# Linear attention into a gated unit: sixteen small gate tiles, and q maxima subtracted without a mask

## The chip, the cores and the metric

The kernel runs on one core of a Trainium2 chip. The core has a matrix engine (TensorE, PE in the profile; its weight loads are shown apart as PEld), VectorE (DVE), ScalarE (ACT), GpSimd (POOL) and SyncE (SP), which here only issues transfers. The metric is the device time of one execution in microseconds (us), the median of several runs.

## The reference

The inputs are q, k and v of 8 batches, 8 heads, 576 positions and 64 channels, and a projection `w_phi` to 128 features. The first half is attention without a softmax over positions; the second half is a gated unit with a causal convolution of five taps over positions, whose 512 channels are the heads side by side.

```python
def phi(x):
    proj = np.einsum('bhsd,df->bhsf', x, w_phi)
    proj = proj - np.max(np.abs(proj), axis=-1, keepdims=True)
    return np.concatenate([np.exp(proj), np.exp(-proj)], axis=-1)
q_p, k_p = (phi(q), phi(k))
kv = np.einsum('bhsf,bhsd->bhfd', k_p, v)
z = np.sum(k_p, axis=2)
num = np.einsum('bhsf,bhfd->bhsd', q_p, kv)
den = np.einsum('bhsf,bhf->bhs', q_p, z)[..., None] + 1e-06
...
for k in range(K):
    gate_pre += conv_w[k][None, None, :] * xp[:, k:k + S, :]
gate = 1.0 / (1.0 + np.exp(-gate_pre))
val = x @ w_val
return (gate * val @ w_out).astype(np.float32)
```

## The kernel before

The batches run one after another through a chain of steps, and the steps of neighbouring batches overlap. Two positions (an even and an odd one) stand on the two halves of the 128 partitions, so most matmuls use 64 rows, in pairs on the two row halves. The 18 blocks of 128 positions and heads of a batch are taken in five units, four of four blocks and one of two (`UNITS`).

The steps of a batch, with the tiles they write:

- Loads: k and q go through `KQN` and a transposing transfer into `kT` and `qT` (batches 0 and 1: through TensorE, lines 537 and 556, with casts at 543, 545 and 561). v goes to `VN`. A one-element copy on GpSimd (`hold`, line 510) waits for the last q block of batch 0, and the loads behind it on GpSimd's queue wait with it.
- k: `kp` projects a unit (line 578), VectorE takes the maxima of the magnitudes (586, into `MK`), ScalarE the two exponentials (596, into `KTIL`). `ek` (605) makes the factors exp of plus and minus the maximum, and `vs` (611 and 612, GpSimd) multiplies v by them, into `VT`, with a column of factors for the denominator: four instructions of 18 x 64 elements a batch, one for each group of heads and sign. `st` (621) sums key features times scaled v into a state, `kv` evicts it (629 or 633, into `KV`).
- q: `qm` projects (578), VectorE takes maxima into `MQP` (586). `mqt` transposes them (663), `mqr` copies them negated into `MQR` (671). `rx` (683, GpSimd) spreads them over a mask of the identity, into `RX`. `qp` projects again (694) and adds, as a second matmul with weights of ones, `RX` (699), so that the maxima are subtracted in PSUM. ScalarE then takes the exponentials (707 and 710, into `QTIL` and `QTT`).
- `num` multiplies q features with the state (720, 727), `nrm` divides (738, 741, into `XN`), and x is transposed into `XT` (749, 753; in the last two batches by a transfer).
- The gated unit works on blocks j of 128 channels. `gate` (782) makes the convolution as matmuls with small diagonal matrices of taps, `GW`: for each tap four matmuls of 64 x 64 tiles, on two row halves and two column halves, for even and odd positions (`par`) in two PSUM banks. ScalarE takes a tanh (786, into `TH`). `val` (792) is the value matmul, `gv` (798) joins the two, and `out` (814, 818) multiplies with `WOUT`; the results are evicted by ScalarE (635) or VectorE (631) and written by SyncE.

Order is written out by hand in tables: `ORDER` lists the steps of all engines in the order in which they are issued, `FLEX` says for each step that can run on two engines which it takes, `BANKS` gives PSUM banks to groups. `WARM` and `ZERO` put extra matmuls into TensorE's stream: full-width ones on ones, and ones with weights of zero that add nothing to a unit's PSUM (line 505). The durations in `build` were for making these tables; they do not act on the chip.

Of the kernel before, what the change touches and what calls it, by code (L numbers as in the profile page):

```python
# [10 lines left out]
ALU = mybir.AluOpType  # L11
# [6 lines left out]
F = 128  # L18
# [6 lines left out]
NU = len(UNITS)  # L25
PEB = 1
QPART = ((0, 1), (2, 3, 4))
# [83 lines left out]
def dve(n, ov=0.075):  # L111
    return n / 960.0 + ov


def act(n):
    return n * 0.000833 + 0.067


class Plan:
    def __init__(self):  # L120
        self.tasks, self.groups = [], []

    def group(self, kind, nb):
# [35 lines left out]
def parts(b):  # L159
    return QPART if b == 0 else (tuple(range(NU)),)  # L160


def build(plan, em=None):
# [11 lines left out]
    def G(*k):  # L175
        return h.get(k)
# [725 lines left out]
```

## Time and profile before

| what | us |
|---|---|
| runs | 216.41, 217.7, 218.19 |
| median | 217.7 |
| span of the profiled execution | 216.2 |
| busy PE, ACT, DVE, POOL | 194.8, 180.8, 170.1, 133.1 |

The profiled execution has no time of its own beside its span; the lowest run is 0.2 us above that span, and the median 1.5 us. Busy time is the union of the instructions' times: matmuls overlap, and each counts with its whole latency, so that PE's busy share says more than its work. A row of the costliest groups gives line, engine, operation, output and inputs with their shape and the number of instructions, then busy time, mean duration in ns, and the idle time just before them with what ended it. A row of the timeline gives start, length and what ran, with like neighbours merged into one piece.

### The profile page before, as it was taken

Reading aid. Unit: us, or ns where it says so; the run is one execution under the profiler, and the core shown is the slowest. Engines: PE = TensorE matmul, PEld = TensorE weight load, DVE = VectorE, ACT = ScalarE, POOL = GpSimd, SP = SyncE. Lnnn points to the kernel's source line nnn. Section 1 sums busy time; section 2 is a strip of 40 time slices with the busy share of each in tenths; the row PEclk is TensorE's granted clock in tenths of the full one; section 3 lists DMA queues with packets and bytes.
Section 4 is the critical chain, followed back from the end, with each engine's and each line's share of the span. In section 5 each row is a group of like instructions: output and inputs, shape, how many; then the busy total and the mean of one; then the engine's idle time right before and its main releaser. Section 6 shows DMA issues by size and latency. Waiting matters only on the chain.

```text
span 216.2 us, 9004 instructions
## 1 busy us (share of the span) xinstructions
PE 194.8 (90%) x3924; PEld 139.5 (65%) x3944; DVE 170.1 (79%) x257; ACT 180.8 (84%) x267; POOL 133.1 (62%) x173
## 2 busy tenths in 40 slices
PE   2987978778999999998999999999999999899990
PEld 2665566566666776676857777568757766687740
DVE  2289999999599988997899978998699897654510
ACT  3689999999999899998999997999988988634251
POOL 3045999997894749961998099902993779210010
PEclk9999999999999999999999999999999999999998
DMA  6999999899599699979998968969953264774166
GB/s 180 380 242 208 306 169 238 154 195 196 111 167 299 115 137 235 300 138 184 220 311 150 137 137 233 199 141 178 296 190 89 62 163 129 85 169 94 49 193 198
DMA packets 49106, 39.86 MB, mean 184 GB/s; under 512 B 33637, under 2 KB 38565, under 8 KB 49066
## 3 DMA queue, kind: packets, MB, share of 16 engines
q1 hardware_dynamic: 42768, 28.58, 57.0%
q0 software_dynamic: 6032, 10.49, 26.1%
q8 instruction: 31, 0.51, 0.9%
q10 hardware_dynamic: 266, 0.21, 0.3%
q14 instruction: 9, 0.07, 0.1%
HBM read 30.48 MB, written 9.44 MB: 185 GB/s over the span
## 4 chain that ended last, share of the span: by engine, by line
PE 55%; ACT 22%; DVE 14%; issue 4%; DMA 2%; SPq 0%; DVEq 0%; ACTq 0%
PE PS L792 11%; PE PS L814 9%; ACT QTIL L707 9%; PE PS L782 9%; ACT KTIL L596 8%; DVE MQP L586 6%; PE PS L720 5%; PE PS L578 5%; PE PS L621 4%; DVE MK L586 3%; DMA KTIL<-in_k_dram 2%; PE PS L694 2%; PE PS L537 2%; PE PS L818 2%; PE PS L699 2%
## 5 line engine op out<-in xcount | busy, mean ns | idle before, releaser
L596 ACT ACTIVATE KTIL<-PS 128x1024 bf16<-128x1024 f32 (+1 forms) x80 | 71.8, 966 | 3.9 <-PE PS L578 1.7
L611 POOL TENSOR_TENSOR VT<-VN,EK 128x1152 bf16<-128x1152 f32 x32 | 67.9, 2121 | 3.3 <-ACT EK L605 3.2
L707 ACT ACTIVATE QTIL<-PS 128x1024 bf16<-128x1024 f32 x64 | 62.6, 1053 | 1.9 <-PE PS L699 1.5
L683 POOL TENSOR_TENSOR RX<-MQR,ident 128x512 bf16<-128x512 bf16 (+1 forms) x39 | 36.6, 961 | 36.7 <-DVE MQR L671 26.1
L586 DVE TENSOR_REDUCE MK<-PS 128x8 f32<-128x1024 f32 (+1 forms) x40 | 44.2, 1112 | 3.5 <-PE PS L578 1.7
L586 DVE TENSOR_REDUCE MQP<-PS 128x8 bf16<-128x1024 f32 (+1 forms) x40 | 43.7, 1112 | 2.7 <-PE PS L578 1.2
L792 PE MATMUL PS<-XT,WV 128*128 128x288 bf16 x256 | 34.8, 286 | 0.3 <-DVE GV L798 0.2
L798 DVE SCALAR_TENSOR_TENSOR GV<-TH,PS 128x576 bf16<-128x576 bf16 x32 | 23.8, 752 | 10.4 <-PE PS L792 4.7
L814 PE MATMUL PS<-WOUT,GV 128*128 128x512 bf16 x110 | 29.7, 380 | 1.1 <-issue 0.2
L792 PEld LDWEIGHTS <-WV 128*128 128x128 bf16 x256 | 23.8, 98 | 7.9 <-issue 1.4
L786 ACT ACTIVATE TH<-PS 128x576 bf16<-128x576 f32 x32 | 20.3, 664 | 8.9 <-PE PS L782 8.7
L621 PE MATMUL PS<-VT,KTIL 64*128 64x65 bf16 x1152 | 23.0, 191 | 0.8 <-issue 0.7
L782 PE MATMUL PS<-XT,GW 64*64 64x288 bf16 x640 | 23.0, 285 | 0.6 <-DVE RCP L738 0.5
L741 DVE TENSOR_TENSOR XN<-PS,RCP 128x512 bf16<-128x512 f32 x32 | 22.1, 691 | 1.2 <-DMA XT<-XN 0.2
L621 PEld LDWEIGHTS <-KTIL 64*128 64x128 bf16 x1152 | 20.7, 95 | 3.3 <-issue 2.3
L720 PEld LDWEIGHTS <-QTIL 128*128 128x128 bf16 x512 | 18.3, 97 | 6.4 <-issue 4.0
L720 PE MATMUL PS<-KV,QTIL 128*128 128x65 bf16 x512 | 20.3, 193 | 0.3 <-DVE MQP L586 0.2
L782 PEld LDWEIGHTS <-GW 64*64 64x64 bf16 x640 | 17.9, 106 | 3.0 <-issue 0.6
L635 ACT ACTIVATE OUTS<-PS 128x512 f32<-128x512 f32 x22 | 13.6, 621 | 7.3 <-PE PS L814 6.1
L814 PEld LDWEIGHTS <-GV 128*128 128x128 bf16 x128 | 11.2, 98 | 11.3 <-issue 0.6
L578 PE MATMUL PS<-W,qT 64*128 64x128 bf16 x288 | 15.4, 219 | 3.1 <-ACT QTIL L707 1.0
L578 PEld LDWEIGHTS <-qT 64*128 64x128 bf16 x288 | 10.8, 95 | 9.4 <-issue 4.6
(80 smaller groups left out, 236.0 us busy)
## 6 DMA issues: line engine op xcount, KB each, us to landing
out_dram<-OUTS SPq DMA_DIRECT2D x32, 256.0 KB, 3.3
VN<-in_v_dram SPq DMA_DIRECT2D x7, 1152.0 KB, 6.5
KQN<-in_q_dram POOLq DMA_DIRECT2D x6, 576.0 KB, 8.2
KQN<-in_k_dram POOLq DMA_DIRECT2D x6, 576.0 KB, 9.0
KTIL<-in_k_dram SPq DMA_DIRECT2D x4, 288.0 KB, 4.2
VN<-in_v_dram POOLq DMA_DIRECT2D x1, 1152.0 KB, 10.2
KTIL<-in_q_dram SPq DMA_DIRECT2D x4, 256.0 KB, 4.4
out_dram<-OUTS SPq DMA_DIRECT2D x14, 64.0 KB, 2.5
```

The lines of the kernel that those rows point to most:

```text
L578: nc.tensor.matmul(self.PS[:, t.grp.banks[par], i * P:(i + 1) * P], X[rows, (c0 + i) * P:(c0 + i + 1) * P], self.W2[rows, :], start=True, ...
L586: self.nc.vector.tensor_reduce(o, self.two(t.grp, n * P).rearrange("p a (c f) -> p a c f", f=F), AX.X, ALU.max, apply_absolute_value=True)
L596: self.nc.scalar.activation(self.KTIL[b % 2][:, s, c0:c0 + n, :, :].rearrange("p c a f -> p a c f"), self.two(t.grp, n * P).rearrange("p a ...
L611: nc.gpsimd.tensor_tensor(self.VT[g][:, s, :, 0:D], self.VN[b % 2][:, NC * g:NC * g + NC, :], e.to_broadcast([P, NC, D]), ALU.mult)
L621: nc.tensor.matmul(self.PS[:, t.grp.banks[ab], (s * 2 + x) * E1:(s * 2 + x + 1) * E1], self.KTIL[b % 2][rows, s, J // 2, J % 2, :], self.V ...
L683: self.nc.gpsimd.tensor_tensor(o, *wide(self.MQR[self.mq(b, u)][:, :], self.ident2), ALU.mult)
L707: self.nc.scalar.activation(o, i, AF.Exp, scale=1.0 - 2.0 * s)
L720: nc.tensor.matmul(self.PS[:, t.grp.banks[h // 4], (h % 4) * E1:(h % 4 + 1) * E1], Q[:, s, c % 2, h, (c // 2) * P:(c // 2 + 1) * P], self. ...
L782: self.nc.tensor.matmul(self.PS[o * D:(o + 1) * D, t.grp.banks[par], 0:R], self.GW[r, jj, 4 - m, :], X[r, 4 * a + jj, :, HALO - 8 * s:HALO ...
L792: self.nc.tensor.matmul(self.PS[:, t.grp.banks[par], 0:R], self.WV[:, i, (2 * j + par) * D:(2 * j + par + 2) * D], X[:, 4 * par + i, :, HA ...
L798: nc.vector.scalar_tensor_tensor(out=self.GV[b % 3][:, j, :, :], in0=self.TH[j][:, :, :], scalar=1.0, in1=self.two(t.grp, R), op0=ALU.add, ...
L814: nc.tensor.matmul(self.PS[:, t.grp.banks[0], :], GV[:, j, c % 2, (c // 2) * XH:(c // 2) * XH + P], self.WOUT[:, c % 2, j, :], start=(j == ...
```

## The change

Five parts, and new tables.

1. `gate` works on two channel blocks at once. Each tap is now sixteen matmuls of 32 x 32 tiles, on four row strips and four column strips, for two blocks (`z`) and even and odd positions (`par`); each (z, par) has its own PSUM bank, so a double gate holds four banks. The channels of a block come out rotated by 32 for odd blocks and by 64 for odd positions, and the value and output weights are rotated to match: `WVE` and `WVO` are rotated copies of the value weights, made by four GpSimd copies, and `WOUT` is loaded in three transfers instead of one, with two copies within the chip instead of three.
2. `rx` and its tile are gone. `qp` subtracts the maxima by four narrow matmuls (two in the last unit) on each row half: the moving operand is `MQR` itself, and the weights are one column of the identity read with a stride of zero, which picks one row of `MQR` for all 128 outputs.
3. `vs` is cut by key half x instead of by sign: one instruction scales 9 positions by both factors. `st` of a half waits for its own `vs` alone. It may run on VectorE; one of 32 does.
4. `mqr` may run on ScalarE; two of nine do.
5. `ZERO` is empty: the 150 matmuls with zero weights are gone. `WARM` now puts six full-width matmuls at the very start, and four later.

```diff
 WARM = (
-    "60:6:1 81:1:1 87:7:2 134:7:1 141:7:1 "
+    "2:6:6 103:0:2 161:3:1 185:3:1 "
 )
-ZERO = "35:76:7 61:80:5 75:34:1 101:105:1 126:215:8 144:223:1 155:192:4 158:200:1 175:315:6 189:346:1 195:241:2 197:241:2 211:327:1"
+ZERO = (
+    ""
+)
 ORDER = (
-    "1 2 9 3 4 11 5 6 10 21 22 19 20 13 12 46 25 26 7 8 23 24 14 27 28 42 29 32 30 33 44 49 76 31 15 43 45 47 16 158 159 48 "
+    "1 2 9 10 3 4 0 11 21 22 32 12 33 46 47 5 6 42 44 45 76 27 28 7 8 77 13 15 48 17 19 20 30 14 43 23 24 25 26 50 16 54 49 "
...
     def c_wv(self, t):
-        self.nc.gpsimd.dma_start(self.WV[:, :, 0:DM], self.wts[0].rearrange("(i p) o -> p i o", p=P))
-
-    def c_wvx(self, t):
-        self.nc.gpsimd.tensor_copy(self.WV[:, :, DM:DM + D], self.WV[:, :, 0:D])
+        self.nc.gpsimd.dma_start(self.WV[:, :, :], self.wts[0].rearrange("(i p) o -> p i o", p=P))
+
+    def c_wvx(self, t, odd):
+        cp = self.nc.gpsimd.tensor_copy
+        W = self.WV[:, :, :].rearrange("p i (w z c) -> p i w z c", w=2, z=2)[:, :, :, odd, :]
+        if odd:
+            cp(self.WVO[:, :, :, 0:96], W[:, :, :, 32:P])
+            cp(self.WVO[:, :, :, 96:192], W[:, :, :, 0:96])
+        else:
+            cp(self.WVE[:, :, :, 0:D], W[:, :, :, D:P])
+            cp(self.WVE[:, :, :, D:P], W[:, :, :, 0:D])
...
-    def vs(self, t, b, g, s):
-        nc = self.nc
-        e = self.EK[:, s, NC * g:NC * g + NC].unsqueeze(2)
+    def vs(self, t, b, g, x):
+        nc = self.nc
+        eng = nc.gpsimd if t.eng == "POOL" else nc.vector
+        r = slice(9 * x, 9 * x + 9)
+        e = self.EK[:, :, NC * g + 9 * x:NC * g + 9 * x + 9].unsqueeze(3)
+        v = self.VN[b % 2][:, NC * g + 9 * x:NC * g + 9 * x + 9, :].unsqueeze(1)
         with nc.allow_low_precision("bf16 scaled v"):
-            nc.gpsimd.tensor_tensor(self.VT[g][:, s, :, 0:D], self.VN[b % 2][:, NC * g:NC * g + NC, :], e.to_broadcast([P, NC, D]), ALU.mult)
-            nc.gpsimd.tensor_copy(self.VT[g][:, s, :, D:E1], e)
+            eng.tensor_tensor(self.VT[g][:, :, r, 0:D], v.to_broadcast([P, 2, 9, D]), e.to_broadcast([P, 2, 9, D]), ALU.mult)
+            eng.tensor_copy(self.VT[g][:, :, r, D:E1], e)
...
-        o = self.RX[u][:, :, 0:n, :]
-        if t.eng == "POOL":
-            self.nc.gpsimd.tensor_tensor(o, *wide(self.MQR[self.mq(b, u)][:, :], self.ident2), ALU.mult)
...
     def qp(self, t, b, u):
...
-        for par in range(2):
-            rows = slice(par * D, (par + 1) * D)
-            nc.tensor.matmul(self.PS[:, t.grp.banks[par], 0:n * P].rearrange("p (h y x) -> p h y x", h=2 * H, y=n),
-                             self.ONES[rows, 0:F], self.RX[u][rows, :, 0:n, :], start=False, stop=True, skip_group_check=True)
+        for y in range(n):
+            for par in range(2):
+                rows = slice(par * D, (par + 1) * D)
+                o = self.PS[:, t.grp.banks[par], 0:n * P].rearrange("p (h y x) -> p h y x", h=2 * H, y=n)
+                nc.tensor.matmul(o[:, :, y, :], self.ident2[rows, c0 + y:c0 + y + 1].to_broadcast([D, F]),
+                                 M[rows, :].rearrange("p (h x) -> p h x", h=2 * H), start=False, stop=True, skip_group_check=True)
...
-    def gate(self, t, b, j):
+    def gate(self, t, b, w):
         X = self.XT[b % 2]
         for m in range(5):
-            for h2 in range(2):
-                r = slice(h2 * D, (h2 + 1) * D)
-                for par in range(2):
-                    o = (h2 + par) % 2
-                    back = m - par
-                    s, a, jj = (back + 1) // 2, back % 2, (j + (par > h2)) % 4
-                    self.nc.tensor.matmul(self.PS[o * D:(o + 1) * D, t.grp.banks[par], 0:R], self.GW[r, jj, 4 - m, :],
-                                          X[r, 4 * a + jj, :, HALO - 8 * s:HALO - 8 * s + XH], start=(m == 0), stop=(m == 4))
+            for z, par in ((0, 0), (1, 0), (0, 1), (1, 1)):
+                j = 2 * w + z
+                bank = (t.grp, t.also)[z].banks[par]
+                back = m - par
+                s, a = (back + 1) // 2, back % 2
+                for i in range(4):
+                    o = (i - 2 * par - z) % 4
+                    r = slice(32 * i, 32 * i + 32)
+                    self.nc.tensor.matmul(self.PS[32 * o:32 * o + 32, bank, 0:R], self.GW[r, j, 4 - m, :],
+                                          X[r, 4 * a + j, :, HALO - 8 * s:HALO - 8 * s + XH], start=(m == 0), stop=(m == 4))
```

The tables move work in all engines. First place: the start of GpSimd's queue, from the `hold` copy (written to `HOLD`) on, before:

```order
L510 CAST HOLD_76<-KTIL1_73 128x1
L551 DMA QTIL1_75<-in_q_dram 128x2304
L551 DMA QTIL1_75<-in_k_dram 128x4x576
L551 DMA KQN1_65<-in_q_dram 128x2304
L551 DMA KQN0_64<-in_k_dram 128x4x576
L683 TENSOR_TENSOR RX1_135<-MQR0_90,ident2_130 128x512
L683 TENSOR_TENSOR RX0_134<-MQR0_90,ident2_130 128x512
L532 DMA VN1_67<-in_v_dram 128x4x576
L611 TENSOR_TENSOR VT0_82<-VN0_66,EK_86 128x18x64
L612 CAST VT0_82<-EK_86 128x18
```

The same place now:

```order
L544 DMA VN1_67<-in_v_dram 128x4x576
L522 CAST HOLD_76<-KTIL1_73 128x1
L563 DMA QTIL1_75<-in_q_dram 128x2304
L563 DMA QTIL1_75<-in_k_dram 128x4x576
L563 DMA KQN1_65<-in_q_dram 128x2304
L563 DMA KQN0_64<-in_k_dram 128x4x576
L626 TENSOR_TENSOR VT0_82<-VN0_66,EK_86 128x2x9x64
L627 CAST VT0_82<-EK_86 128x2x9
```

The load of batch 1's v went from behind two `rx` to ahead of the hold, with nothing but memsets before it; the `rx` are gone.

Second place: the start of ScalarE, casts of k and q of batch 0 (`kT0`, `qT0`) and the first exponentials (`KTIL0`), before:

```order
L456 DMA cw5_141<-in_moe_conv_w_dram 5x512
L545 ACT_TABLE_LOAD
L545 CAST kT0_68<-PS_63 128x512 x3
L596 ACTIVATE KTIL0_72<-PS_63 128x2x4x128 x2
L545 CAST qT0_70<-PS_63 128x512
```

And now:

```order
L454 DMA cw5_141<-in_moe_conv_w_dram 5x512
L557 ACT_TABLE_LOAD
L557 CAST kT0_68<-PS_63 128x512
L557 CAST qT0_70<-PS_63 128x512
L608 ACTIVATE KTIL0_72<-PS_63 128x2x4x128 x3
```

Two casts of k went to VectorE here, one cast of q came ahead of the exponentials; in all, ScalarE has five of these ten casts instead of nine.

Third place: ScalarE after the last q exponentials (`QTT`), with the tanh of the last two batches (`TH`), before:

```order
L710 ACTIVATE QTT_81<-PS_63 128x8x32 x4
L635 ACTIVATE OUTS7_118<-PS_63 128x512
L786 ACTIVATE TH3_105<-PS_63 128x576
L786 ACTIVATE TH2_104<-PS_63 128x576
L786 ACTIVATE TH0_102<-PS_63 128x576
L633 COPY XT1_101<-PS_63 128x16x16
L786 ACTIVATE TH1_103<-PS_63 128x576
```

And now:

```order
L714 ACTIVATE QTT_81<-PS_63 128x8x32 x4
L648 COPY XT0_103<-PS_63 128x16x16
L650 ACTIVATE OUTS7_121<-PS_63 128x512
L792 ACTIVATE TH3_108<-PS_63 128x576
L792 ACTIVATE TH2_107<-PS_63 128x576
L792 ACTIVATE TH1_106<-PS_63 128x576
L792 ACTIVATE TH0_105<-PS_63 128x576
```

The last transposed piece of batch 6's x is now copied here too, and the tanh come in pairs, as two are fed by one double gate. Behind the last q exponential TensorE had eight gates, eight value groups and nine output groups; now it has four double gates, eight value groups and eleven output groups.

More of the change, by code (lines that the diff above doesn't have):

```diff
@@ L116, in act, with parts @@
     return n * 0.000833 + 0.067
+def parts(b):
+    return QPART if b == 0 else (tuple(range(NU)),)
 class Plan:
@@ L224, in build @@
                 cx = A("lk", 0, 0, "DMA", 3.7, None, [cl], rank=-450)
-                cx = A("wvx", 0, 0, "POOL", 0.4, fn("c_wvx"), [cx], rank=-440)
-                cx = A("wvx", 0, 0, "DMA", 0.0, None, [cx], rank=-440)
+                cx = [A("wvx", 0, i, "POOL", 1.4, fn("c_wvx", i), [cx], rank=-440) for i in range(2)]
             last = [xf["q"], xf["k"]]
@@ L249, in build @@
             cc = A("mqt", 0, 0, "DVE", 0.2, fn("c_cw2"), [cc], g, rank=-500)
[L250 to L252 removed]
+            cg = A("mqt", 0, 0, "POOL", 1.3, fn("c_gt"), [cc], rank=-10)
             for j in range(4):
[L254 to L255 removed]
+                h["val", 0, j].deps.append(cx[j % 2])
+            for j in (0, 2):
+                h["gate", 0, j].deps.append(cg)
         ld = h["lv0",] = A("lv", b, 0, "POOL" if b == 1 else "SP", 0.65, fn("loadv", b),
@@ L276, in build @@
         for gi in range(2):
-            for s in range(2):
-                h["vs", b, gi, s] = A("vs", b, gi, "POOL", 2.22, fn("vs", b, gi, s),
-                                      [eks[gi % len(eks)], G("lv", b)] + [G("st", b - 1, gi, x) for x in range(2)])
+            for x in range(2):
+                h["vs", b, gi, x] = A("vs", b, gi, ("POOL", "DVE"), (2.22, 1.36), fn("vs", b, gi, x),
+                                      [eks[gi % len(eks)], G("lv", b), G("st", b - 1, gi, x)])
             g = plan.group("st", 2)
@@ L335, in build @@
         xall = [G("xtc", b, i) for i in range(3)] + [halo]
-        for j in range(4):
-            g = plan.group("gate", 2)
-            gt = h["gate", b, j] = A("gate", b, j, "PE", 0.62, fn("gate", b, j), xall, g, 3)
-            h["tanh", b, j] = A("tanh", b, j, "ACT", act(576), fn("tanh", b, j), [gt, G("gv", b - 1, j)], g)
+        for w in range(2):
+            gs = [plan.group("gate", 2) for _ in range(2)]
+            gt = A("gate", b, w, "PE", 0.66, fn("gate", b, w), xall, gs[0], 3, also=gs[1])
+            for i in range(2):
+                j = 2 * w + i
+                h["gate", b, j] = gt
+                h["tanh", b, j] = A("tanh", b, j, "ACT", act(576), fn("tanh", b, j), [gt, G("gv", b - 1, j)], gs[i])
         for j in range(4):
@@ L404, in __init__ @@
         self.MQR = TT("MQR", 3, [P, P])
+        for m in self.MQP:
+            nc.gpsimd.memset(m[:, :], 0.0)
         self.KV = TT("KV", 2, [P, 2, 2, 2, 2, E1])
```

89 lines of the change are left out of this document (39 added, 50 removed), and 67 rows, old and new, of the table ORDER.

## The prediction

> **What bounds the kernel now.** I read the page's totals first, then the chain of work that ended last, then busy time by stretch, then ScalarE's waits, and last the tail.
>
> ```profile
> span 216.2 us, 9004 instructions
> PE 194.8 (90%) x3924; PEld 139.5 (65%) x3944; DVE 170.1 (79%) x257; ACT 180.8 (84%) x267; POOL 133.1 (62%) x173
> PE 55%; ACT 22%; DVE 14%; issue 4%; DMA 2%; SPq 0%; DVEq 0%; ACTq 0%
> ```
>
> The chain is more than half TensorE (PE), and GpSimd (POOL) is not in it. Busy time by stretch (columns: length, then PE, weight loads, VectorE, ScalarE, GpSimd):
>
> ```profile
> 13.00:43.00 30.00, 24.12 (x543) 17.63 (x540) 28.30 (x37) 28.89 (x45) 24.27 (x26) 1.00 1.05 214
> 100.00:186.00 86.00, 84.99 (x1758) 59.65 (x1768) 75.50 (x116) 78.69 (x117) 60.95 (x74) 1.00 0.79 170
> 186.00:217.00 31.00, 24.44 (x349) 17.00 (x350) 11.57 (x21) 11.43 (x21) 2.18 (x8) 0.96 0.57 136
> ```
>
> Three regimes. Up to 43 us ScalarE and VectorE are full (28.9 and 28.3 of 30) and PE has room. From 100 to 186 us PE is full (85.0 of 86), ScalarE at 78.7, VectorE at 75.5: all close to their limit, PE first. From 186 us ScalarE has only 11.4 us left and PE finishes alone. What ScalarE waits for between 20 and 186 us (releaser, us in total, times, longest):
>
> ```profile
> ACT TH L786 <- PE PS L782: 2.0, 4, 0.6
> ACT QTIL L707 <- PE PS L699: 1.5, 3, 1.0
> ACT KTIL L596 <- PE PS L578: 1.4, 2, 1.0
> ACT QTT L710 <- PE PS L699: 1.3, 1, 1.3
> ```
>
> So ScalarE is fed late by PE, but these four rows are only 6.2 us together: that is nearly all that a faster PE can give before 186 us, because behind PE stands a ScalarE that already works 9 us in 10.
>
> **The change, part by part.**
>
> *Gates.* First the pitch. A merged piece of n passes lasts (n - 1) pitches and one duration.
>
> ```profile
> L782 PE MATMUL PS<-XT,GW 64*64 64x288 bf16 x640 | 23.0, 285 | 0.6 <-DVE RCP L738 0.5
> 163.57 1.42 PE L782 MATMUL PS<-XT,GW 64*64 64x288 bf16 x40
> 195.94 3.26 PE L782 MATMUL PS<-XT,GW 64*64 64x288 bf16 x100
> ```
>
> x40 is ten passes of four tiles: (1.42 - 0.285) / 9 = 0.126 us a pass; x100 gives (3.26 - 0.285) / 24 = 0.124. Four tiles side by side cost one stream of 288 columns. A gate is 5 passes, 0.63 us; 32 of them take 20.2 us of PE. If sixteen tiles also go side by side, two gates cost 5 passes: 16 x 0.63 = 10.1 us, and 10.1 us of PE goes. Lower bound of the gain: one instruction stream must issue 160 instructions in 0.63 us.
>
> ```profile
> L621 PE MATMUL PS<-VT,KTIL 64*128 64x65 bf16 x1152 | 23.0, 191 | 0.8 <-issue 0.7
> 184.59 1.32 PE L621 MATMUL PS<-VT,KTIL 64*128 64x65 bf16 x72
> ```
>
> The densest stream before is this one: (1.32 - 0.191) / 35 = 0.032 us for two matmuls and two weight loads, 8.1 ns an instruction. If that is a limit of issue, a double gate takes 160 x 8.1 = 1.29 us, and nothing is gained. But 65 columns of streaming explain most of the 32 ns (a pass of 288 in 0.124 us would make it 28), so I take the full gain. How it reaches the end: before 186 us only through ScalarE's 6.2 us of waits. PE also hands over later in places that the rows don't blame, so I take half: -3.1, with ends 0 and -6.2.
>
> The Trainium skill (TensorEngine Tiling (Array Packing), Gotcha 1: PSUM Pressure) says that different row tiles can't access one PSUM bank at the same time. By that rule the four row tiles that the new gate puts into each bank would take turns, and the gain would be a loss (rival D). The rows speak against it: in the old gate two row halves already write different partitions of one bank, at one stream's cost.
>
> *q maxima.* Each unit's one 512-column matmul per row half becomes four of 128 columns, 288 new matmuls less 80 old ones, each with its weight load.
>
> ```profile
> L699 PE MATMUL PS<-RX,ONES 64*128 64x512 bf16 x64 | 12.3, 375 | 0.0
> 13.17 0.39 PE L578 MATMUL PS<-W,qT 64*128 64x128 bf16 x8
> L578 PE MATMUL PS<-W,qT 64*128 64x128 bf16 x80 | 4.3, 216 | 2.4 <-ACT QTIL L707 1.0 <-ACT qT L545 0.8 <-DVE MQP L586 0.4
> L578 PEld LDWEIGHTS <-qT 64*128 64x128 bf16 x288 | 10.8, 95 | 9.4 <-issue 4.6
> ```
>
> The nearest row is the projection with the same shape: (0.39 - 0.216) / 3 = 0.058 us a pair. Old: 12.3 / 32 = 0.38 at most a full unit, 0.22 where pipelined behind its first half; new: 4 x 0.058 = 0.23. Some 0.3 us over the run; I take 0. A stride of zero in a weight load is in no row. Bounds: 0, and all 144 pairs of loads exposed, 144 x 0.095 = 13.7 us of PE. I take the low end, since the loads of the projection hide entirely at that pitch.
>
> *GpSimd.* It loses the masks and keeps 31 of 32 scalings.
>
> ```profile
> L683 POOL TENSOR_TENSOR RX<-MQR,ident 128x512 bf16<-128x512 bf16 (+1 forms) x39 | 36.6, 961 | 36.7 <-DVE MQR L671 26.1
> L611 POOL TENSOR_TENSOR VT<-VN,EK 128x1152 bf16<-128x1152 f32 x32 | 67.9, 2121 | 3.3 <-ACT EK L605 3.2
> ```
>
> 36.6 us leave an engine that is 62% busy and not in the chain: 0 by itself. It shortens the path from q maxima to q exponentials by about 1 us a unit, which is part of the half taken above. The state matmul of a half now waits for one scaling of 2.1 us, not two. The four new copies of the rotated value weights ride in the time freed.
>
> *ScalarE and VectorE.* By counting: ScalarE loses four casts of early q/k (two of 512, two of 256 columns), three output evictions (in the tail) and one 1024-wide copy, and gains two state evictions and two small q-maxima copies.
>
> ```profile
> L545 ACT CAST kT<-PS 128x512 bf16<-128x512 f32 x4 | 2.3, 584 | 2.4 <-PE PS L537 2.4
> L633 ACT COPY XT<-PS 128x1024 bf16<-128x1024 bf16 x2 | 2.1, 1047 | 0.0
> L633 ACT CAST KV<-PS 128x520 bf16<-128x520 f32 x4 | 2.5, 628 | 0.3 <-PE PS L621 0.3
> L545 ACT CAST kT<-PS 128x256 bf16<-128x256 f32 x1 | 0.4, 372 | 0.3 <-PE PS L537 0.3
> L671 DVE TENSOR_SCALAR MQR<-PS 128x128 bf16<-128x128 bf16 x7 | 1.5, 219 | 0.8 <-PE PS L663 0.8
> ```
>
> Before the last q exponential: -2 x 0.58 - 2 x 0.37 - 1.05 + 2 x 0.63 + 2 x 0.22 = -1.3 us; ScalarE is the next bound, so I take -1.2 (ends -1.3 and, if the small copies cost as much as a 256-wide one, -0.9). VectorE gains about as much, and one of the 32 scalings; it has 10 us free in 100 to 186 us, but almost none before 43 us.
>
> *Start.* Gone are the padding matmuls with zeros. Two groups stand in the chain:
>
> ```profile
> 12.05 1.29 PE PS L505 x28
> 17.49 0.56 PE PS L505 x20
> GB/s 180 380 242 208 306 169 238 154 195 196 111 167 299 115 137 235 300 138 184 220 311 150 137 137 233 199 141 178 296 190 89 62 163 129 85 169 94 49 193 198
> 19.12 0.81 POOL L532 DMA_DIRECT2D VN<-in_v_dram  x1
> VN<-in_v_dram POOLq DMA_DIRECT2D x1, 1152.0 KB, 10.2
> ```
>
> Up to 1.29 + 0.56 = 1.85 us; the next work was partly held by VectorE, so -1.2. Against it: the v load of batch 1, issued at 19.12 us before, now stands first on GpSimd's queue, ahead of the hold that keeps loads back until batch 0's q is in. Nothing delays it; it goes out by about 3 us and shares the engines with the first k and q. 1152 KB at the 380 GB/s of the second slice is 3.1 us: between 0 and +3.1, and I take +1.5, half, since the two queues share.
>
> *Tail.* After the last q exponential stood 8 gates and 9 output groups; now 4 double gates and 11.
>
> ```profile
> 204.09 3.24 PE PS L814 x15
> ...
> 210.13 1.00 PE PS L818 x8
> ```
>
> Gates: 8 x 0.63 becomes 4 x 0.63, -2.5. Two output groups more: one of four matmuls, 4 x 3.24 / 15 = 0.86, and one of eight, 1.00: +1.9. Net -0.6, between -2.5 (they fit into gaps) and 0 (the sixteen tiles take longer to start).
>
> **Sum**, on the profiled execution: -3.1 - 1.2 - 1.2 + 1.5 - 0.6 = -4.6, from 216.2 to 211.6. The lowest run, 216.41, is 0.2 above that span, the median of 217.7 is 1.5 above it; the forecast for the median is 217.7 - 4.6 = 213.1 us. Its own range, with each term moved by half its way: 209 to 216.
>
> **The rivals.** About 1%, 2.2 us, is what a measurement of this kernel can tell from no change.
>
> B, the change doesn't do what it says: issue limits the double gate to 1.29 us. PE gains nothing, the -3.1 goes, the tail gets +2.0: -1.2 - 1.2 + 1.5 + 2.0 = +1.1, 218.8. For it: the 8.1 ns row. Against it: tiles that start together in the pass of four.
>
> C, all comes through: -6.2 - 1.85 - 1.3 - 2.5 and the load hidden: -11.9, 205.8. For it: PE has 85.0 of 86 us in the middle, and is freed there. Against it: every engine would have to mesh.
>
> D, slower: the row tiles take turns in a bank. A double gate then takes 4 x 0.63 = 2.5 us, 1.25 more than two gates now. Where the gates lie, by stretch (PE busy with line 782, and its matmuls):
>
> ```profile
> 0.00:40.00 40.00, 0.00 (x0) 0.00 (x0) 1.00 0.99 240
> 40.00:80.00 40.00, 6.17 (x160) 4.40 (x160) 1.00 0.98 178
> ```
>
> 480 of 640, twelve double gates of sixteen, fall after 80 us, where PE leads: 12 x 1.25 = +15, and without the gain 217.7 + 1.1 + 15 = 234. It turns slower than before by over 1% once a double gate takes more than about 1.35 us. The rows of the old gate are against it. Under the Trainium skill (TensorE: Matmul & The Clock Gate, "Wait — 56ns, not 53.3ns?") matmuls never start closer than about 25 ns apart; 80 of them would then take 2.0 us, the same rival at a smaller price. The 72 matmuls in 1.32 us disagree.
>
> E, PE cools without the padding.
>
> ```profile
> L578 PE MATMUL PS<-W,kT 64*128 64x128 bf16 x16 | 1.0, 306 | 0.0
> L505 PE MATMUL PS<-ONES,NIL 64*128 64x128 bf16 x126 | 5.2, 220 | 0.0
> ```
>
> The projections before 12.8 us took 306 ns each, after it 216: the array ran slower until the first padding. If it stayed so up to 43 us, (24.1 - 5.2) x (306 / 216 - 1) = 7.9 us of PE are added there, under ScalarE's cover; half of it lands: 213.1 + 4 = 217.1. Six warming matmuls now at the very start speak against it.
>
> F, weight loads with zero stride are exposed: PE gets 13.7 - 10.1 = 3.6 more, the -3.1 turns to about +3.6: 213.1 + 6.7 = 219.8.
>
> **Chances.** Forecast 0.54, C 0.12, B 0.13, E 0.09, F 0.06, D 0.05, 0.01 left. The range 206.5 to 219.5 leaves out D, half of F, and half of C: about 0.14, with the far ends of the rest under 0.2. Faster by over 1% (below 215.5): most of the forecast, C and some of E, 0.67. Within 1%: the forecast's slow end, most of B and E: 0.21. Slower: D, F and some of B, 0.12.
>
> **What would show it.** A double gate as one piece of 80 matmuls in about 0.9 us, its last latency included; 0.06 us a pair in the selector rows; ScalarE's waits for PE before the last q exponential at about half; the first transposes not later than 4 to 5 us; projections at 216 ns after 13 us; GpSimd near 100 us busy. If double gates take over 1.3 us, or the first k lands after 6 us, the forecast is wrong at that step.

## The result: slower by a ninth, and the profile after

The changed kernel takes 242.55 us (four runs, 240.81 to 244.14) where the kernel before took 217.62 beside it: a ratio of 1.112 with an interval of 1.105 to 1.120. The forecast was 213.1, so it lies on the other side. Ratios, here and below, are against the kernel before run beside each version, and leave out runs over 1.5% above the fastest of the same kernel; medians and ranges hold all runs. The profiled execution spans 240.7 us, 24.5 more than before. Lines of its page (totals, granted clock by slice, the queue of instruction fetches with packets and MB, shares of the chain):

```profile
span 240.7 us, 10367 instructions
...
PE 199.3 (83%) x4628; PEld 142.1 (59%) x4646; DVE 174.7 (73%) x262; ACT 178.2 (74%) x263; POOL 99.1 (41%) x136
...
PEclk9859985795899988999999999988979999999998
...
q8 instruction: 36, 0.59, 1.0%
...
PE 53%; issue 14%; DVE 10%; ACT 10%; DMA 7%; POOL 4%; DVEq 0%; POOLq 0%; ACTq 0%
```

The page of the kernel before had in the same place:

```profile
q8 instruction: 31, 0.51, 0.9%
```

VectorE works 4.6 us longer than before, ScalarE 2.6 us less, GpSimd 34 us less. What is new in the chain is "issue", 14% of the span where it was 4%: time in which the engine of the chain waits for nothing that the profile shows. About half of its 34 us is TensorE (PE) standing still, as shown below; its longest piece, 6.83 us from 221.96 us on, isn't, since PE works in it. And the array's clock, full before from 13 to 214 us, dips in several places. Both show in a stretch of the chain of work (start, length, what ran) and in busy time by stretch (columns as in the prediction; the granted clock is the third number from the end):

```profile
52.40 0.62 PE PS L788 x35
53.02 2.90 issue
55.92 0.93 PE PS L788 x39
...
84.94 3.75 issue
...
110.78 1.65 issue
...
116.43 1.37 issue
...
157.08 4.38 issue
...
171.16 2.07 issue
```

```profile
34.40:44.60 10.20, 7.80 (x133) 5.60 (x128) 9.18 (x13) 9.26 (x12) 6.43 (x10) 0.50 0.82 117
...
55.00:61.70 6.70, 5.78 (x214) 4.72 (x215) 2.28 (x4) 3.36 (x8) 0.00 (x0) 0.50 0.59 139
61.70:85.00 23.30, 21.73 (x554) 15.85 (x553) 19.33 (x30) 22.43 (x34) 11.53 (x15) 1.00 0.83 153
85.00:89.00 4.00, 0.31 (x20) 0.31 (x22) 1.77 (x2) 0.69 (x1) 0.00 (x0) 1.00 1.18 195
89.00:92.40 3.40, 3.18 (x37) 1.87 (x31) 0.47 (x1) 2.53 (x3) 1.54 (x3) 0.50 1.03 278
```

The first stall stands in the middle of a double gate: 39 of its 80 matmuls are out, nothing is missing, and for 2.90 us nothing is issued. After it the array runs at half clock for 6.7 us; after the stall of 3.75 us, for 3.4. So a long stall is paid twice. (The first row, 34.4 to 44.6 us, is the stretch that has lost its padding; no stall of this kind stands ahead of it.)

Where do they stand? I numbered all of PE's weight loads and matmuls in the trace in order, with the few semaphore instructions among them. The eight stalls of the changed kernel have the numbers 1470, 3005, 4025, 4281, 6069, 6581, 7604 and, a short one, 1982: modulo 256 that is 190, 189, 185, 185, 181, 181, 180 and 190, drifting down as the trace loses records. In the traces further below in which no matmul record is missing, every such stall, 18 of them in three kernels, is at 193 modulo 256. They are the ends of blocks of 256 instructions. The queue above moves just such blocks, 0.59 MB / 36 = 16.4 KB each. Its packets, beside the moments at which PE enters a block:

| PE enters a block | packet with the next block | PE at that block's start | stands |
|---|---|---|---|
| 49.5 | 53.27 to 54.39 | 53.02 | to 55.92 |
| 82.5 | 86.31 to 87.33 | 84.94 | to 88.69 |
| 97.6 | 100.30 to 101.23 | 102.5 | no |
| 153.7 | 159.17 to 160.15 | 157.08 | to 161.46 |
| 182.6 | 184.32 to 185.25 | 187.1 | no |

Only one block ahead is on its way: its packet starts 0 to 5.5 us after PE enters the one before (2.1 in the mean for blocks entered between 30 and 160 us, the packets taken in order, one for each block), takes about 1.0 us, and after a stall PE goes on 1.3 to 1.6 us after its end. A block that PE gets through faster than that ends in a stall. A double gate is 160 of the 256 instructions. But gates aren't the only bursts: three of the eight blocks that ended in a stall, with 9.1 of the 17.7 us (3.75, 4.38 and 0.99), hold no gate at all. Over 100 of their 128 matmuls are state matmuls (`st`), and PE was through them in 2.4 to 3.4 us; the packets behind the two long stalls started late, 3.8 and 5.4 us after the block was entered.

The idle time of PE by kind (stalls over 0.3 us from 15 us to the last output, summed from the instruction records; the runs are told of below):

| kernel | time | at block ends | elsewhere | PE busy |
|---|---|---|---|---|
| before | 217.6 | 1.4 | 5.2 | 194.8 |
| after | 242.6 | 17.7 | 7.5 | 199.3 |
| after, 64x64 gates | 232.2 | 7.2 | 12.5 | 196.1 |
| before, gates split | 227.0 | 7.8 | 6.0 | 196.3 |
| before, selector | 221.0 | 3.6 | 5.8 | 194.4 |
| before, few loads | 216.6 | 0.0 | 5.7 | 194.5 |
| after, few loads | 225.6 | 6.4 | 8.2 | 193.1 |
| after, 64x64 gates, few loads | 224.2 | 0.6 | 8.8 | 196.7 |

Of the 24.5 us of span, 16.3 are stalls at block ends, 2.3 other stalls, and 4.5 more busy time, although the gates themselves got shorter: the array is at half clock in 27 of the us behind 17. The rest, 1.4 us, lies ahead of 15 us.

The lines that the prediction had named, after the change: what ScalarE waits for (20 to 211 us), and three pieces of PE's timeline, the late block of k among the first transposes, a double gate, and a unit's selector:

```profile
ACT KTIL L608 <- PE PS L590: 8.4, 6, 3.0
ACT TH L792 <- PE PS L788: 6.8, 4, 3.5
ACT QTIL L711 <- PE PS L703: 6.1, 11, 1.6
```

```profile
11.55 1.33 PE L549 MATMUL PS<-ident_f,KTIL 128*128 128x128 f32 x5 [2.48 <-DMA KTIL<-in_k_dram]
...
113.20 1.05 PE L788 MATMUL PS<-XT,GW 32*32 32x288 bf16 x80
...
121.17 0.39 PE L703 MATMUL PS<-MQR,ident 64*128 64x128 bf16 x8
```

ScalarE's waits did not halve: these three rows alone are 21.3 us where four were 6.2 (20 to 186 us then). The double gate takes 1.05 us, less than the 1.42 of two old gates and more than the 0.9 that the prediction named. The selector is as cheap as forecast. The first transposes started in time, at 3.99 us, but one of the later blocks of k came 2.5 us late.

### The profile page after: what moved, and what is told of

Read it like the earlier page. It is cut to its first block, busy times and chain, and to the rows that moved or that the text cites. A ratio compares the mean times of both kernels' runs of the same rounds, so it can differ in the third digit from the quotient of the medians.

```text
span 240.7 us, 10367 instructions
## 1 busy us (share of the span) xinstructions
PE 199.3 (83%) x4628; PEld 142.1 (59%) x4646; DVE 174.7 (73%) x262; ACT 178.2 (74%) x263; POOL 99.1 (41%) x136
## 4 chain that ended last, share of the span: by engine, by line
PE 53%; issue 14%; DVE 10%; ACT 10%; DMA 7%; POOL 4%; DVEq 0%; POOLq 0%; ACTq 0%
PE PS L798 10%; PE PS L820 8%; PE PS L636 7%; PE PS L788 6%; ACT KTIL L608 5%; PE PS L724 5%; PE PS L590 5%; DVE MQP L598 4%; PE PS L696 3%; DMA KTIL<-in_k_dram 3%; POOL VT L626 3%; PE PS L703 2%; PE PS L753 2%; DMA qT<-KQN 2%; ACT QTIL L711 2%
## 5 line engine op out<-in xcount | busy, mean ns | idle before, releaser
L626 POOL TENSOR_TENSOR VT<-VN,EK 128x1152 bf16<-128x1152 f32 x31 | 65.7, 2120 | 44.0 <-ACT EK L617 21.2
L820 PE MATMUL PS<-WOUT,GV 128*128 128x512 bf16 x113 | 31.5, 394 | 6.2 <-issue 5.1
L636 PE MATMUL PS<-VT,KTIL 64*128 64x65 bf16 x1152 | 24.8, 195 | 5.7 <-issue 4.7
L788 PE MATMUL PS<-XT,GW 32*32 32x288 bf16 x1280 | 19.1, 300 | 4.0 <-issue 2.9
L650 ACT ACTIVATE OUTS<-PS 128x512 f32<-128x512 f32 x19 | 11.5, 615 | 13.5 <-PE PS L820 6.7
L798 PE MATMUL PS<-XT,WVO 128*128 128x288 bf16 x128 | 18.7, 288 | 1.5 <-issue 1.4
L646 DVE TENSOR_SCALAR OUTS<-PS 128x512 f32<-128x512 f32 x17 | 11.6, 686 | 11.0 <-PE PS L820 10.2
L788 PEld LDWEIGHTS <-GW 32*32 32x32 bf16 x1280 | 13.2, 88 | 9.1 <-issue 6.4
L590 PE MATMUL PS<-W,kT 64*128 64x128 bf16 x288 | 15.8, 230 | 2.6 <-ACT KTIL L608 1.1
L696 PE MATMUL PS<-qT,W 64*128 64x512 bf16 (+1 forms) x80 | 15.7, 387 | 1.8 <-DVE MQP L598 0.5
```

Source lines behind the costliest of these rows:

```text
L590: nc.tensor.matmul(self.PS[:, t.grp.banks[par], i * P:(i + 1) * P], X[rows, (c0 + i) * P:(c0 + i + 1) * P], self.W2[rows, :], start=True, ...
L626: eng.tensor_tensor(self.VT[g][:, :, r, 0:D], v.to_broadcast([P, 2, 9, D]), e.to_broadcast([P, 2, 9, D]), ALU.mult)
L636: nc.tensor.matmul(self.PS[:, t.grp.banks[ab], (s * 2 + x) * E1:(s * 2 + x + 1) * E1], self.KTIL[b % 2][rows, s, J // 2, J % 2, :], self.V ...
L696: nc.tensor.matmul(self.PS[:, t.grp.banks[par], 0:n * P], self.W2[rows, :], X[rows, c0 * P:(c0 + n) * P].rearrange("p (y h x) -> p h y x", ...
L788: self.nc.tensor.matmul(self.PS[32 * o:32 * o + 32, bank, 0:R], self.GW[r, j, 4 - m, :], X[r, 4 * a + j, :, HALO - 8 * s:HALO - 8 * s + XH ...
L798: self.nc.tensor.matmul(self.PS[:, t.grp.banks[par], 0:R], self.wv(i, j, par), X[:, 4 * par + i, :, HALO:XW], start=(i == 0), stop=(i == 3))
```

## The experiments

Theory 1 says: the loss is instruction supply. Its rivals are gates that are slow in themselves, the colder array, the early v load, and the new order.

**Gates as 64x64 tiles** (the changed kernel with half the gate instructions; double gates, order and the rest stay, except that the taps' tile and the rotated copies of the weights are made to match).

```diff
-                for i in range(4):
-                    o = (i - 2 * par - z) % 4
-                    r = slice(32 * i, 32 * i + 32)
-                    self.nc.tensor.matmul(self.PS[32 * o:32 * o + 32, bank, 0:R], self.GW[r, j, 4 - m, :],
+                for i in range(2):
+                    o = (i + par) % 2
+                    r = slice(D * i, D * i + D)
+                    self.nc.tensor.matmul(self.PS[D * o:D * o + D, bank, 0:R], self.GW[r, j, 4 - m, :],
```

> The changed kernel with its tables, selector and scalings, but each double gate made of 64 x 64 tiles again: 40 matmuls in ten passes of four instead of 80 in five passes of sixteen, so 1280 PE instructions fewer and about 0.4 us more streaming a double gate. Theory 1 (instruction supply): the changed kernel stands still where a block of 256 PE instructions is used up before the next block has been fetched; with fewer instructions most of the seven stalls of 1 us and more go, and the array no longer cools after them: 217 to 225 us, clock 0.96 or more. Theory 2 (the missing padding lets the array cool in the first 45 us, and that delays all): little changes, 236 to 246. Theory 3 (the new order of steps is itself bad): the longer gates make it worse, 244 to 252.

232.24 us (230.35 to 233.54), ratio 1.061 [1.053, 1.070]. 10 us come back, between the theories. In the profiled execution, 8.9 us shorter, the stalls at block ends fall by 10.5 us, to 7.2, and PE's busy time by 3.2, while other stalls grow by 5.0. 14 us are left for other parts.

**The kernel before, each 64x64 gate matmul split into its two diagonal 32x32 blocks.** Same result, same order, 1280 more instructions.

```diff
+                    for e in range(0, D, 32):
+                        r = slice(h2 * D + e, h2 * D + e + 32)
+                        self.nc.tensor.matmul(self.PS[o * D + e:o * D + e + 32, t.grp.banks[par], 0:R], self.GW[r, jj, 4 - m, e:e + 32],
```

> The kernel before, all tables as they were, with each 64 x 64 gate matmul split into its two 32 x 32 blocks on the diagonal (the other blocks of a tap's weights are zero): the same ten passes a pair of gates, eight tiles in each instead of four, 1280 PE instructions more, no streaming more. Theory 1: PE now runs out of instructions at ends of blocks of 256, with stalls of 1 to 4 us in which nothing is waited for: 224 to 240 us. Theories 2 and 3 (padding, order): nothing they blame is touched, 217 to 219.

227.01 us (225.88 to 231.25), ratio 1.039 [1.033, 1.045]. Nothing but the number and the size of the gate's matmuls has changed, and 8 to 9 us are gone. Of the 8.6 us by which the profiled span is longer, 6.4 are stalls at block ends; gates that are slow in themselves are at most a small part, their rows being busy for 25.6 us where they were for 23.0. Timeline of PE (idle time in brackets): the same signs as after the change.

```profile
53.20 0.43 PE L784 MATMUL PS<-XT,GW 32*32 32x288 bf16 x13 [1.47 <-issue]
76.82 0.78 PE L784 MATMUL PS<-XT,GW 32*32 32x288 bf16 x33 [1.01 <-issue]
...
104.41 0.57 PE L720 MATMUL PS<-KV,QTIL 128*128 128x65 bf16 x13 [1.25 <-issue]
108.41 0.43 PE L784 MATMUL PS<-XT,GW 32*32 32x288 bf16 x15 [1.25 <-issue]
```

**The changed kernel, shifted by 120 instructions** (64 one-column matmuls in place of four warming ones at the start).

```diff
-    "2:6:6 103:0:2 161:3:1 185:3:1 "
+    "2:6:2 103:0:2 161:3:1 185:3:1 "
+            if i == 2:
+                for _ in range(64):
+                    nc.tensor.matmul(em.PS[0:32, 6, 0:1], em.ONES[0:32, 0:32], em.ONES[0:32, 0:1], start=True, stop=True)
```

> The changed kernel with 120 PE instructions more at its start, where PE waits for the first load anyway: 64 matmuls of one column in place of four of the six warming ones. Theory 1: the stalls stay at every 256th instruction of the stream, so they come 120 instructions earlier in the program, at other steps; 234 to 248 us. Theories 2 and 3, or a wait that the profile doesn't show: they stay at the same steps of the program (ahead of the first double gate, and so on), 241 to 244.

243.97 us in one run. The time stays, and the stalls keep their place in the count, not in the program: the first long one now falls into a state matmul, the next into another gate, at the numbers 1726, 1982 and 2749, which are 190, 190 and 189 modulo 256.

```profile
59.14 0.73 PE L636 MATMUL PS<-VT,KTIL 64*128 64x65 bf16 x19 [4.06 <-issue]
63.14 0.66 PE L788 MATMUL PS<-XT,GW 32*32 32x288 bf16 x17 [0.66 <-issue]
84.53 0.65 PE L788 MATMUL PS<-XT,GW 32*32 32x288 bf16 x17 [2.35 <-issue]
```

**The early v load put back** behind the loads of k and q.

```diff
+            if t.kind == "lv" and t.b == 1 and t.fn is not None:
+                held = t
+                continue
...
+            if t.kind == "lk" and t.b == 2 and t.fn is not None:
+                held.fn(held)
```

> The changed kernel with the load of batch 1's v behind the four loads of k and q on GpSimd's queue, as it was before, instead of ahead of the hold. Theory 3, as far as the early load goes: the pause of 2.5 us in which PE waits for k near 9 us goes, and the run is 1 to 3 us shorter, 239.5 to 241.5. Theory 1: at most that, since the stalls come later; if later loads delay a block of instructions elsewhere it can also be 240 to 245.

241.82 us (239.69 to 245.34), ratio 1.105 [1.097, 1.113] where the changed kernel has 1.112 [1.105, 1.120]: 0.7 us under its median, within the spread. The 2.5 us wait for k goes; how much of that reaches the end can't be told from these runs, and neither can the theories be told apart by them.

**64x64 gates and the old way with the maxima** (GpSimd's multiplication follows directly on `mqr`; 416 fewer instructions still).

```diff
+        for u in parts(b)[i]:
+            c0, n = UNITS[u]
+            self.nc.gpsimd.tensor_tensor(self.RX[u][:, :, 0:n, :],
...
-        for y in range(n):
-            for par in range(2):
...
+        for par in range(2):
+            rows = slice(par * D, (par + 1) * D)
+            nc.tensor.matmul(self.PS[:, t.grp.banks[par], 0:n * P].rearrange("p (h y x) -> p h y x", h=2 * H, y=n),
+                             self.ONES[rows, 0:F], self.RX[u][rows, :, 0:n, :], start=False, stop=True, skip_group_check=True)
```

> The changed kernel with its gates as 64x64 tiles again and with the q maxima subtracted as before (GpSimd multiplies maxima by the identity, one wide matmul a half subtracts them): 7523 rows of TensorE instructions, against 7939 with 64x64 gates alone, 9219 after and 7817 before. Theory 1 (the time goes with the number of instructions that TensorE has to be supplied with, and most where they stand densely): 416 fewer instructions, at 10 us for the 1280 that the gates gave up, take 3 us or a little more: 224 to 230 us, and TensorE's idle time at the ends of 256-instruction blocks falls below the 9 us of the run with 64x64 gates. Theory 2 (what is left of the loss, 14 us, is the new order, the early load of v and the missing padding): 231 to 236 us, since GpSimd gets 34 us of work back and nothing else changes.

264.04 us (262.83 to 265.92): both theories missed. The stalls at block ends did fall, to 3.9 us, but PE's longest waits are others:

```profile
PE PS L558 <- DMA QTIL<-in_q_dram: 7.7, 1, 7.7
PE PS L695 <- POOL RX L680: 7.4, 6, 2.8
PE PS L626 <- POOL VT L617: 6.4, 5, 3.3
```

The multiplications stand ahead of the loads of batch 1 in GpSimd's queue. The run says nothing about the selector; it says that this order counts on a GpSimd without that work.

**The selector alone, in the kernel before** (with `rx` empty).

```diff
-        for par in range(2):
...
-                             self.ONES[rows, 0:F], self.RX[u][rows, :, 0:n, :], start=False, stop=True, skip_group_check=True)
+        for y in range(n):
+            for par in range(2):
...
+                nc.tensor.matmul(o[:, :, y, :], self.ident2[rows, c0 + y:c0 + y + 1].to_broadcast([D, F]),
```

> The kernel before with the zero-stride selector alone (288 small matmuls in place of 80 wide ones, GpSimd's multiplication left away): 416 more TensorE instructions, 34 us less GpSimd work. Theory 1 (instructions cost by their number, 9 us for 1280 in the kernel before): 219.5 to 223 us. Theory 2 (the selector costs what its rows say, 0.06 us a pair beside ScalarE, and removes a GpSimd step ahead of the q projections): 214 to 218 us.

221.02 us (219.65 to 221.65), ratio 1.011 [1.004, 1.018]: 2.3 us slower, as theory 1 has it. The selector's matmuls cost nothing on PE (194.4 us busy against 194.8), GpSimd loses 36 us of work, and still 416 instructions more cost time: stalls at block ends are 3.6 us where they were 1.4. Two of them:

```profile
81.26 0.59 PE L816 MATMUL PS<-WOUT,GV 128*128 128x512 bf16 x2 [0.83 <-issue]
95.62 0.30 PE L621 MATMUL PS<-VT,KTIL 64*128 64x65 bf16 x8 [1.53 <-issue]
```

**Fewer loads**, first v of batches 2 to 7, in both kernels:

```diff
     def loadv(self, t, b):
+        if b > 1:
+            return
```

> The changed kernel without the loads of v for batches 2 to 7 (the v of batches 0 and 1 is used again, so the output is another; some 7 of 38 MB less traffic). Theory 1 (the next block of instructions comes by a transfer that queues behind the data of the same DMA engines, so with less data it lands sooner after TensorE has entered the block before): 230 to 237 us, the mean lag from entering a block to the start of the fetch of the next one, 2.2 us between 30 and 175 us after the change, falls below 1.6 us, and the idle time at block ends falls by 5 us or more. Theory 2 (the lag is not one of DMA load, or the loss is elsewhere): 239 to 243 us, and the lag stays at 2 us or more.

> The kernel before without the loads of v for batches 2 to 7, as the control of the run beside it (again another output). Theory 1: the kernel before stands still for instructions only once, for 0.7 us, so less data gives it 0 to 2 us: 215 to 218 us. Theory 2 (what less data gives to the changed kernel it gives by data that arrive earlier, not by instructions): the same gain as in the changed kernel, whatever it is.

After: 234.75 us (230.32, 232.45, 237.06 and 238.1), ratio 1.059 [1.048, 1.070] by the two shorter runs. Before: 217.13 us (216.17 to 220.07), ratio 0.994 [0.991, 0.998]. The changed kernel gains some 8 us by the medians and 11 by the ratios, the one before 1: as theory 1 expects of the time. Two of its numbers fail in the profiled execution, which is the longest of the four: the lag, 2.1 us, became 1.9 and not under 1.6, and the stalls at block ends fell by 2.3 us, from 17.7 to 15.3, and not by 5.

Then also k and q of batches 3 to 7, in both:

```diff
     def load(self, t, w, b):
+        if b > 2:
+            return
```

> The changed kernel without the loads of k and q for batches 3 to 7 and of v for batches 2 to 7 (earlier data are used again, so the output is another); the outputs are still stored. Theory 1 (the fetch of the next 256 instructions waits behind data in the DMA engines): with the engines nearly free between 60 and 170 us the mean lag from entering a block to the start of the next fetch, 2.7 us after the change, falls to 1.2 us or less, the idle time at block ends from 17.7 to under 8 us, and the time to 222 to 231 us. Theory 2 (the lag is the fetch's own, whatever the DMA engines do): lag over 2 us, idle at block ends over 13 us, 235 us or more.

> The kernel before without the same loads, as the control. Theory 1: little to gain, since only 2 us are lost at block ends: 213 to 217 us, so that the changed kernel's distance to it falls from 25 to 7 to 16 us. Theory 2: the distance stays at 18 us or more.

After: 225.63 us (224.4 to 228.96), ratio 1.030 [1.024, 1.036]. Before: 216.64 us (215.69 to 217.55), ratio 0.993 [0.989, 0.996]. The distance shrinks from 25 to 9.0 us. The page of the changed kernel without these loads:

```profile
span 223.2 us, 10349 instructions
...
PE 193.1 (87%) x4646; PEld 137.6 (62%) x4646; DVE 174.0 (78%) x262; ACT 177.5 (80%) x263; POOL 91.9 (41%) x126
...
PEclk9769999589999999999999999999999999999997
```

The control, the kernel before without them:

```profile
span 213.8 us, 8991 instructions
...
PE 194.5 (91%) x3944; PEld 137.7 (64%) x3944; DVE 170.6 (80%) x257; ACT 180.3 (84%) x267; POOL 126.1 (59%) x163
```

The changed kernel's span is 17.5 us shorter than with all loads, the control's 2.4. Stalls at block ends fall by 11.3 us and PE's busy time by 6.2 (the clock no longer dips after 50 us); other stalls stay. So not late data, but late instructions and the cold array behind them had cost it: waits for data would be among the other stalls. The lag falls to 1.2 us, as theory 1 expected (from 2.1 to 1.0 in the kernel before). The 2.7 us in the expectation is too long: it gave one block, whose packet starts 0.1 us before PE enters it, the packet of the block behind it.

**The padding**, put back into the changed kernel (`ZERO` filled, behind 21 projections) and taken out of the kernel before (`ZERO` empty).

```diff
-    ""
+    "81:91:2 82:82:2 95:192:2 98:209:2 103:94:2 112:213:2 114:184:2 125:100:2 130:176:2 139:188:2 144:207:2 149:180:2 151:211:2 156:296:2 162:300:2 167:215:2 173:327:2 176:219:2 178:331:2 183:333:2 186:222:2"
```

> The changed kernel with zero matmuls put back behind 21 projections between some 25 and 45 us (304 more rows of TensorE instructions), where its array clock had halved from 34.4 to 44.6 us. Theory 1 (the clock there costs little, since ScalarE and VectorE are busy for 30 of the 32 us; the loss lies in later block ends): the granted clock is full in that stretch, and the time 240 to 247 us. Rival E of the prediction (the array cools without the padding, and that carries the loss): 232 to 238 us.

> The kernel before without its 150 zero matmuls (7517 rows of TensorE instructions in place of 7817). Theory 1 (300 instructions less, as 1280 more cost 9 us; the cooling costs little under ScalarE's and VectorE's work): 214.5 to 218.5 us. Rival E: the array cools before 45 us as it does after the change, and the time is 220 to 224 us.

Put back: 237.46, 242.39, 244.35 and 244.83 us, too far apart for a verdict. The lowest lies in rival E's range, the other three in theory 1's, and the profile is of one of those, 244.35 us. Taken out: 219.87 us (217.9 to 220.92), ratio 1.004 [1.000, 1.008], between the two theories: about 0.9 us slower. The clock rows, of the changed kernel with padding and of the kernel before without:

```profile
PEclk9997999997799976999799997999999899999999
```

```profile
PEclk9996999589999999999999999999999999999999
```

With padding the clock is full from 23 to 57 us, but the time of this execution doesn't follow; what the padding is worth in the changed kernel stays open, between nothing and some 5 us. In the kernel before without it the array does cool before 45 us, and that costs little: ScalarE and VectorE, not PE, were full in that stretch.

**64x64 gates with few loads.** What is left here is not supply.

> The changed kernel with 64x64 gates and without the loads of k and q for batches 3 to 7 and of v for batches 2 to 7 (earlier data are used again, so the output is another). Its control is the kernel before without these loads, 216.6 us. Theory 1 (the 14 us that were left with 64x64 gates are instruction supply like the rest): with the fetch early it takes 216 to 221 us, with under 2 us of idle time at block ends. Theory 2 (they are the new order: waits for other engines and the longer start): 224 to 230 us, with 10 us or more of idle time elsewhere.

224.17 us (223.57 to 225.26), ratio 1.030 [1.024, 1.035]: theory 2 in the time, 7.5 us over the control. Block ends cost 0.6 us; other stalls are 8.8 us (10 or more were expected) against 5.7, and PE's busy time is 2.2 us longer. Beside the changed kernel with few loads, the groups of the gate, first as 64x64, then as 32x32:

```profile
L781 PE MATMUL PS<-XT,GW 64*64 64x288 bf16 x640 | 23.4, 285 | 1.2 <-POOL GW L488 0.7 <-DVE MQP L591 0.2
```

```profile
L792 PE MATMUL PS<-XT,GW 32*32 32x288 bf16 x1280 | 18.7, 287 | 2.0 <-issue 1.0 <-ACT QTIL L715 0.3 <-ACT KV L652 0.2
```

The sixteen tiles do save PE time, 4.7 us in these rows, 3.6 in its whole busy time (196.7 and 193.1). But even with few loads they add 5.8 us of stalls at block ends, and in time the kernels with and without them can't be told apart: both stand at a ratio of 1.030.

No version of the changed kernel here beats the kernel before.

## Why the prediction was wrong

**The step that failed** is the first, the gates: "Lower bound of the gain: one instruction stream must issue 160 instructions in 0.63 us." It asked how fast PE can issue instructions that it has. It didn't ask how fast it gets them, and so put that cost at nothing without a reason; it is 16.3 us of stalls at block ends more than before, with stretches at half clock behind the longest. Signs of it stood in the profile of before: 31 packets on the instruction queue, the share of "issue", and a stall of 0.70 us in the middle of a stream (97.18 us, number 3515, 187 modulo 256). The change adds 1404 matmuls and weight loads (702 of each, by the PEld counts of the two pages), five and a half blocks, and puts 1280 of them into sixteen bursts. PE was through the eight blocks that ended in a stall in 2.4 to 4.4 us; five of them hold such bursts, the other three mostly state matmuls. No rival had this.

The Trainium skill (Runtime: NRT & Kernel Launch, "Instruction fetch mechanics") says that instructions come in blocks of 16 KiB, 256 each, the next one while the current runs, at a cost "mostly hidden". Block size and the one block ahead agree with the stalls' period and the packets of 16.4 KB; the cost does not: here it is 17.7 us, in stalls of up to 4.4.

How the 24.9 us split, by the runs: some 16 go with the loads (24.9 less the 9.0 between the kernels with few loads): late fetches and the halved clock behind them. In what is left the sixteen tiles can't be told from 64x64 ones. 7.5 us remain with few loads and 64x64 gates, where block ends cost only 0.6; of the 8.0 us between the two profiled spans there, 3.1 are other stalls of PE, 2.2 its busy time, and some 2 lie ahead of 15 us. The missing padding is 0.9 of it as measured in the kernel before, and may be more in the changed one. The rest belongs to the new order and the start. Since the order is one table, I didn't try its parts, and what in it costs this is open.

Point by point:

- *Gates.* A piece of 80 matmuls, its last latency included, was to take 0.9 us, and takes 1.05. It saves 1.42 - 1.05 = 0.37 us on two old gates where the sum had 0.63 and B nothing. In PE's busy time over the run that is 3.6 to 4.7 us (between the kernels with few loads) where I took 10.1.
- *Row tiles in one bank* (D): refuted. Four of them write one bank side by side; 1.05 us, not 2.5. The rule of the Trainium skill that the prediction weighed there (TensorEngine Tiling (Array Packing), Gotcha 1: PSUM Pressure) doesn't hold for these tiles, and neither does its 25 ns from start to start (TensorE: Matmul & The Clock Gate, "Wait — 56ns, not 53.3ns?"): 79 starts in 1.05 - 0.29 us are 10 ns apart.
- *Selector.* Right in its rows: (0.39 - 0.228) / 3 = 0.054 us a pair, weight loads hidden, F refuted. Wrong at "I take 0": in the kernel before it costs 2.3 us, and 2.2 us of stalls at block ends came with its instructions.
- *GpSimd.* Right in its time, 99.1 us. But it is in the chain now, with 4%, where it had no part before.
- *ScalarE and VectorE.* ScalarE works 2.6 us less (1.2 forecast before the last exponential); no gain shows, as ScalarE now waits longer for PE.
- *Start.* A k block late by 2.5 us, as feared, but no gain clear of the spread when that was undone. In the kernel before the padding had not cost 1.2 us; it had earned about 0.9.
- *E*, the cooling: it happened (34.4 to 44.6 us). In the kernel before it cost about 0.9 us; in the changed one the runs with padding leave its price open, up to some 5 us. The cold stretches behind 50 us are those that follow the long stalls, and they are gone with few loads. Over the whole run the projections took 229 and 230 ns, not 216.
- *Tail.* From the end of the last q exponential to the end: 30.3 us (240.7 - 210.4) after, 29.4 (216.2 - 186.8) before. No gain; forecast -0.6.

The third that I left for no gain and worse was spread over mechanisms of PE itself. The range had no case in which PE stood still for want of instructions, and so ended at 219.5.

## What to carry to other kernels

Count the instructions of the busiest engine as a cost of its own: where a change makes many small matmuls out of few, work out how long a block of 256 lasts, and compare it with the lag and length of the instruction packets in the trace. Idle time put down to nothing ("issue") in the middle of a stream, at a fixed place in the count of instructions, is the sign. Leaving out loads, with the same done to the old kernel, separates late instructions from slow ones.

## What was not expected of the hardware

- PE had one block of 256 instructions in reserve, no more: its stalls stand at one place of the count (193 modulo 256, 18 of 18), with the next packet started 0 to 5.5 us after the block before was entered. What starts it is open: it comes earlier when data are few (2.1, 1.9 and 1.2 us in the mean with all, fewer and few loads), but not at once.
- Stalls of 2.9 and 3.75 us were followed by 6.7 and 3.4 us at half clock. Shorter ones can be too: 2.06 us after the change and 1.47 us in the kernel before with split gates, by 3.4 us each, while 1.65 and 1.36 us after the change were not.
- Five passes of sixteen tiles take longer than five of four tiles did: 1.05 us for 80 matmuls, where four pitches of 0.125 us and one duration of 0.285 would be 0.79.
- A weight load with a stride of zero costs what others do: 100 ns in the selector's rows after the change, 100 in the projections'.
